# A linear-attention and MoE kernel: TensorE's order fixed by hand, the state product row-tiled, and exp left in PSUM

## The chip, the cores and the metric

The kernel runs on one core of one Trainium2 chip. The metric is the device time in microseconds (us). "Before" is the tuned kernel that the change starts from, "after" is the kernel with the change. A *unit* is one piece of MoE work of about 0.65 us on TensorE: 6 matmuls of 256 columns, 12 of 128 (both for the first MoE product), or 4 of 384 (for the second).

Engines in the profile: PE is TensorE (PEld its weight loads), DVE is VectorE, ACT is ScalarE, POOL is GpSimd, SP is the engine that issues the loads.

## The reference, cut to what matters

```python
# r, k, v, w: (4 batches, 8 heads, 768 positions, 48); u: (8, 48); moe_w_in: (384, 2048); moe_w_out: (2048, 384)
for t in range(S):                                    # attention with a decaying state
    cur = einsum('bhd,bhe->bhde', u[None] * kt, vt)
    y[:, :, t] = einsum('bhd,bhde->bhe', rt, state + cur)
    state = wt[..., None] * state + einsum('bhd,bhe->bhde', kt, vt)
x = y.transpose(0, 2, 1, 3).reshape(3072, 384)
out = square(maximum(x @ w_in, 0)) @ w_out            # fp32 in and out
```

The kernel cuts the sequence into 24 *steps* of 128 positions (4 batches of 6 chunks). Attention must go step by step within a batch. The MoE part of a step can be done at any time after that step's y exists.

## The kernel before

One step of attention is a chain over four engines. The short names are used in all that follows.

| name | engine | what |
|---|---|---|
| Ln, v_bf | ScalarE | logarithm of w; v to bf16 |
| c | TensorE | prefix sums of the logarithms in PSUM |
| exp, rdec | ScalarE, VectorE | exp of c; r and k times their decays |
| ku, qprod, q, vq | GpSimd; q on VectorE | the "bonus" with u; q is a row sum |
| t, rkT | TensorE, VectorE | transposes; eviction of them |
| p, pmT | TensorE, VectorE | scores; two masked evictions |
| s, t_state, S | TensorE, VectorE, GpSimd | state product and state update |
| y, y_sb | TensorE, VectorE | output; eviction with the bonus added |
| x, xT | TensorE, ScalarE | transposes of y; eviction into the MoE's input |

A MoE unit of the first product is evicted by ScalarE (relu, `rl`) and squared by VectorE (`gt`). The parts that the change touches, cut:

```python
def cast_wi(g):
    nc.vector.tensor_copy(wi_sb[:, :, g * GW:(g + 1) * GW], w_st.pop(("i", g))[:])
...
load_wi(0); load_wi(1); load_wi(2); load_wi(3)      # 3 MB of moe_w_in ahead of step 1's inputs
loads[1] = attn_load(1)
...
def st_cum(step):                                   # c, exp, rdec
    ...
    nc.tensor.matmul(cs[:, 0, 0:DM], tri_strict[:], lw[:, :, 0:D], start=True, stop=True)
    nc.tensor.matmul(cs[:, 1, 0:DM], tri_incl_neg[:], lw[:, :, 0:D], start=True, stop=True)
    exps = a_mid.tile([C, 2, H, D], BF16, name="exps")            # exp goes to SBUF
    nc.scalar.activation(exps[:]..., cs[:, :, 0:DM], AF.Exp)
    nc.vector.tensor_mul(rdec[:, :, :, 0:D], st["rk_raw"][:], exps[:])
...
def st_su(step):                                    # state: a 96 x 96 product per pair of heads, masked
    ...
    nc.gpsimd.tensor_mul(am[:], bmask[:], a_c[:, :, None].to_broadcast([C, HP, 2 * D]))
    nc.vector.tensor_add(t_state[:], st["S"][:], su_view)
    nc.gpsimd.tensor_mul(S_new[:], t_state[:], am[:])
...
for t in range(NSTEP):                              # the order is a wish; a scheduler sorts every engine's queue at build time
    ...
    st_prep(t + 1); st_cum(t + 1)
    fill(3); st_p(t); st_bonus(t + 1)
    fill(3); st_tr(t + 1)
    fill(2); st_y(t); st_su(t + 1)
    fill(2); st_yt(t); ready(t); fill(2)            # fill(n): up to n MoE units, if there are any
```

## Time and profile before

Four runs: 237.1, 237.66, 237.76 and 238.68 us. What matters:

| | before |
|---|---|
| span of the profiled run | 235.5 us |
| TensorE busy | 192.9 us (82%) |
| VectorE / ScalarE / GpSimd busy | 165.1 / 126.4 / 118.9 us |
| first MoE matmul | 26.27 us |
| last y transpose | 215.84 us |

The page of the kernel before: busy time by engine; then three rows of its 40 slices of the span (5.9 us each, in tenths busy, and the granted clock in tenths, shown as 9 also where the trace has no clock record yet); then groups of instructions (line, engine, operation, output<-inputs, shapes, count | busy us, mean ns of one | idle time of the engine before them and what ended it).

```profile
PE 192.9 (82%) x1944; PEld 139.2 (59%) x1944; DVE 165.1 (70%) x271; ACT 126.4 (54%) x241; POOL 118.9 (50%) x125
...
PE   0124787889696779969998998999999999999983
...
DVE  3297429999979688486779879788787775753500
...
PEclk9999999999799979967999999999999999999999
...
L277 DVE TENSOR_TENSOR gt<-rl 128x512 bf16<-128x512 f16 x96 | 52.8, 568 | 17.4 <-ACT rl L276 17.0
...
L208 POOL TENSOR_TENSOR am<-bmask,a_c 128x384 f32<-128x384 f32 x20 | 17.2, 858 | 37.2 <-ACT a_c L206 37.2
...
L216 POOL TENSOR_TENSOR S<-t_state,am 128x384 bf16<-128x384 f32 x20 | 23.4, 1168 | 6.1 <-DVE t_state L214 5.4
...
L178 DVE TENSOR_TENSOR rdec_buf_157<-rk_raw,exps 128x768 bf16<-128x768 f32 x8 | 10.6, 1328 | 4.1 <-ACT exps L175 3.3
```

TensorE is full (9, with an 8 now and then) only from the 19th slice on. The state's two GpSimd groups are L208 and L216. One third of the rdec products (L178) took 1328 ns on average; over all 24 they range from 947 to 1745 ns.

The view by stretches of 20 us (columns: stretch; its length; busy time and count of PE, PEld, DVE, ACT, POOL; granted clock; DMA share; GB/s):

```profile
20.00:40.00 20.00, 14.25 (x153) 10.78 (x150) 11.19 (x19) 12.80 (x19) 8.87 (x10) 1.00 1.07 261
40.00:60.00 20.00, 17.12 (x217) 13.14 (x215) 19.47 (x31) 14.14 (x28) 18.04 (x18) 1.00 1.22 180
60.00:80.00 20.00, 17.09 (x164) 11.87 (x164) 17.65 (x27) 10.72 (x22) 14.02 (x14) 0.91 1.11 199
80.00:100.00 20.00, 16.88 (x166) 11.80 (x166) 12.77 (x23) 10.25 (x21) 14.18 (x14) 0.91 0.97 177
100.00:120.00 20.00, 17.56 (x150) 12.22 (x150) 14.86 (x24) 10.26 (x20) 10.52 (x11) 0.83 0.52 106
```

Each stretch of 20 us holds 14 to 17.6 us of busy TensorE, and the granted clock falls to 0.83 in the last.

**How much is lost, and where.** Useful TensorE work is about 176 us: 192 unit equivalents of 0.65 us and 24 steps of 2.1 us (the sum of a step's matmuls, read from the trace). This is an estimate from trace durations. A stretch's loss is its length less the useful work done in it, where a step's 2.1 us are counted whole, when its y transposes run. (To count every matmul at its own start instead moves up to 2.8 us from one stretch to the next.) For the kernel before: 24.2 us until 26.5 us, 9.2 until 50, 5.6 until 80, 12.9 until 130, 7.7 after that; 59.6 in all.

### The profile page before, as it was taken

Reading aid. Unit: us, or ns where it says so; the run is one execution under the profiler, and the core shown is the slowest. Engines: PE = TensorE matmul, PEld = TensorE weight load, DVE = VectorE, ACT = ScalarE, POOL = GpSimd, SP = SyncE. Lnnn points to the kernel's source line nnn. Section 1 sums busy time; section 2 is a strip of 40 time slices with the busy share of each in tenths; the row PEclk is TensorE's granted clock in tenths of the full one; section 3 lists DMA queues with packets and bytes.
Section 4 is the critical chain, followed back from the end, with each engine's and each line's share of the span. In section 5 each row is a group of like instructions: output and inputs, shape, how many; then the busy total and the mean of one; then the engine's idle time right before and its main releaser. Section 6 shows DMA issues by size and latency. Waiting matters only on the chain. (4 is left out here: it accounts for less than half of the span.)

```text
span 235.5 us, 5074 instructions
## 1 busy us (share of the span) xinstructions
PE 192.9 (82%) x1944; PEld 139.2 (59%) x1944; DVE 165.1 (70%) x271; ACT 126.4 (54%) x241; POOL 118.9 (50%) x125
## 2 busy tenths in 40 slices
PE   0124787889696779969998998999999999999983
PEld 0023655658475448646756766678677686776741
DVE  3297429999979688486779879788787775753500
ACT  2203785758376436644654745767566574652710
POOL 4355335898586866747349596783224505200000
PEclk9999999999799979967999999999999999999999
DMA  8999989999999999524694195540101101010101
GB/s 139 339 313 301 334 170 191 170 198 188 173 218 173 203 212 198 119 56 101 130 202 71 43 225 73 114 90 33 36 0 36 36 3 67 0 36 35 34 33 67
DMA packets 107175, 30.40 MB, mean 129 GB/s; under 512 B 100368, under 2 KB 105616, under 8 KB 107152
## 3 DMA queue, kind: packets, MB, share of 16 engines
q1 hardware_dynamic: 107152, 30.09, 62.0%
q8 instruction: 15, 0.25, 0.5%
q14 instruction: 8, 0.07, 0.1%
HBM read 25.36 MB, written 4.72 MB: 128 GB/s over the span
## 5 line engine op out<-in xcount | busy, mean ns | idle before, releaser
L272 PEld LDWEIGHTS <-wi_sb 128*128 128x128 bf16 x624 | 59.0, 102 | 17.5 <-issue 9.6
L277 DVE TENSOR_TENSOR gt<-rl 128x512 bf16<-128x512 f16 x96 | 52.8, 568 | 17.4 <-ACT rl L276 17.0
L287 PEld LDWEIGHTS <-gt 128*128 128x128 bf16 x384 | 36.3, 99 | 23.4 <-issue 4.0
L208 POOL TENSOR_TENSOR am<-bmask,a_c 128x384 f32<-128x384 f32 x20 | 17.2, 858 | 37.2 <-ACT a_c L206 37.2
L166 POOL TENSOR_TENSOR vq<-v_raw,q 128x384 f32<-128x384 f32 x24 | 24.3, 1013 | 22.6 <-DVE y_sb L248 17.5
L230 DVE TENSOR_TENSOR pmT<-cp,tri_strict 128x512 bf16<-128x512 f32 x48 | 30.9, 681 | 4.7 <-PE cp L227 4.7
L161 POOL TENSOR_TENSOR ku<-rk_raw,u_bc 128x384 f32<-128x384 f32 x24 | 26.9, 1121 | 13.8 <-DMA rk_raw<-in_k_dram 9.0
L162 POOL TENSOR_TENSOR qprod<-rk_raw,ku 128x384 f32<-128x384 f32 x24 | 26.4, 1099 | 2.8 <-DVE q L164 1.0
L216 POOL TENSOR_TENSOR S<-t_state,am 128x384 bf16<-128x384 f32 x20 | 23.4, 1168 | 6.1 <-DVE t_state L214 5.4
L175 ACT ACTIVATE exps<-cp 128x768 bf16<-128x768 f32 x24 | 19.5, 813 | 10.6 <-PE cp L173 10.4
L164 DVE TENSOR_REDUCE q<-qprod 128x8 f32<-128x384 f32 x24 | 13.1, 547 | 14.0 <-POOL qprod L162 10.9
L155 ACT CAST v_bf<-v_raw 128x384 bf16<-128x384 f32 x24 | 12.2, 509 | 11.7 <-PE y L244 6.0
L188 DVE COPY rkT<-tr 128x1024 bf16<-128x1024 bf16 x24 | 16.4, 683 | 0.9 <-PE tr L187 0.7
L241 PE MATMUL y<-v_bf,pmT 128*128 128x48 bf16 x192 | 13.9, 187 | 3.6 <-DVE pmT L230 3.5
L256 ACT COPY xT<-y 128x384 bf16<-128x384 bf16 x24 | 11.5, 478 | 8.5 <-PE y L255 7.9
L241 PEld LDWEIGHTS <-pmT 128*128 128x128 bf16 x192 | 11.5, 98 | 6.6 <-DVE pmT L230 5.0
L248 DVE TENSOR_TENSOR y_sb<-vq,y 128x384 bf16<-128x384 f32 x24 | 13.2, 549 | 1.2 <-PE y L244 1.2
L206 ACT ACTIVATE a_c<-su 128x4 f32<-128x4 f32 x20 | 3.4, 170 | 19.6 <-PE su L202 19.6
L178 DVE TENSOR_TENSOR rdec_buf_159<-rk_raw,exps 128x768 bf16<-128x768 f32 x8 | 9.5, 1188 | 5.9 <-ACT exps L175 5.9
L178 DVE TENSOR_TENSOR rdec_buf_157<-rk_raw,exps 128x768 bf16<-128x768 f32 x8 | 10.6, 1328 | 4.1 <-ACT exps L175 3.3
L255 PE MATMUL y<-ident,y_sb 128*128 128x128 bf16 x72 | 8.5, 231 | 5.2 <-DVE y_sb L248 5.1
L227 PE MATMUL cp<-rkT 64*128 64x128 bf16 x192 | 10.5, 231 | 1.8 <-ACT exps L175 1.8
(299 smaller groups left out, 383.9 us busy)
## 6 DMA issues: line engine op xcount, KB each, us to landing
w_raw<-in_w_dram SPq DMA_DIRECT2D x24, 192.0 KB, 4.3
rk_raw<-in_r_dram SPq DMA_DIRECT2D x24, 192.0 KB, 4.3
rk_raw<-in_k_dram SPq DMA_DIRECT2D x24, 192.0 KB, 4.5
v_raw<-in_v_dram SPq DMA_DIRECT2D x24, 192.0 KB, 4.2
out_dram<-o_sb SPq DMA_DIRECT2D x24, 192.0 KB, 2.0
w_st<-in_moe_w_in_dram SPq DMA_DIRECT2D x4, 768.0 KB, 8.1
w_st<-in_moe_w_out_dram SPq DMA_DIRECT2D x4, 768.0 KB, 8.2
u_bc<-in_u_dram SPq DMA_DIRECT2D x1, 192.0 KB, 4.5
```

What stands on the lines that cost most here:

```text
L161: nc.gpsimd.tensor_mul(ku[:], st["rk_raw"][:, 1], u_bc[:])
L162: nc.gpsimd.tensor_mul(qprod[:], st["rk_raw"][:, 0], ku[:])
L166: nc.gpsimd.tensor_mul(vq[:], st["v_raw"][:], q[:, :, None].to_broadcast([C, H, D]))
L175: nc.scalar.activation(exps[:].rearrange("p a h d -> p a (h d)"), cs[:, :, 0:DM], AF.Exp)
L178: nc.vector.tensor_mul(rdec[:, :, :, 0:D], st["rk_raw"][:], exps[:])
L208: nc.gpsimd.tensor_mul(am[:], bmask[:], a_c[:, :, None].to_broadcast([C, HP, 2 * D]))
L216: nc.gpsimd.tensor_mul(S_new[:], t_state[:], am[:])
L230: nc.vector.tensor_mul(pmT[:, e], ps_p[:, e].rearrange("p (a t) -> p a t", a=HP), tri_strict[:, None, :].to_broadcast([C, HP, C]))
L241: nc.tensor.matmul(ps_y[:, h, :], st["pmT"][:, e, p, :], st["v_bf"][:, h, :], start=(h == 0), stop=(c == 0), skip_group_check=True)
L272: nc.tensor.matmul(ps1[:, j, :], wi_sb[:, kk, n * 128:(n + 1) * 128], xT[:, kk, t0:t0 + width], start=(kk == 0), stop=(kk == KT - 1))
L277: nc.vector.tensor_mul(hold["gt"][:, g * ng:(g + 1) * ng, :], rl[:], rl[:])
L287: nc.tensor.matmul(ps2[:], gt[:, n, mt * 128:(mt + 1) * 128], wo_sb[:, n, :], start=(n == 0), stop=(n == NT - 1))
```

## The change

Its intent: keep TensorE fed. TensorE's order is written by hand as a string of stages, with MoE units ("F") between them; the scheduler goes on sorting the other engines. Besides, exp stays in PSUM, the state is kept without its masked half (row-tiled 48-column products), w_in's casts go to ScalarE, and step 1's inputs are loaded before w_in. The core of the diff:

```diff
 def cast_wi(g):
-    nc.vector.tensor_copy(wi_sb[:, :, g * GW:(g + 1) * GW], w_st.pop(("i", g))[:])
+    nc.scalar.copy(wi_sb[:, :, g * GW:(g + 1) * GW], w_st.pop(("i", g))[:])
...
-    load_wi(0) ... load_wi(3)
     loads[1] = attn_load(1)
+    for g in range(4):
+        load_wi(g)
+    loads[2] = attn_load(2)
...
-        exps = a_mid.tile([C, 2, H, D], BF16, name="exps")
-        nc.scalar.activation(exps[:]..., cs[:, :, 0:DM], AF.Exp)
-        nc.vector.tensor_mul(rdec[:, :, :, 0:D], st["rk_raw"][:], exps[:])
+        nc.scalar.activation(a_c[:], cs[:, 0, DM:DM + HP], AF.Exp)
+        nc.scalar.activation(cs[:, :, 0:DM], cs[:, :, 0:DM], AF.Exp)
+        nc.vector.tensor_mul(rdec[:, :, :, 0:D], st["rk_raw"][:], cs[:, :, 0:DM]...)
...
-            nc.tensor.matmul(ps_su[:, p * 2 * D:(p + 1) * 2 * D],
-                             rdec[:, 1, 2 * p:2 * p + 2, :], v_bf[:, 2 * p:2 * p + 2, :], ...)
-        nc.gpsimd.tensor_mul(am[:], bmask[:], a_c[:, :, None].to_broadcast([C, HP, 2 * D]))
-        nc.gpsimd.tensor_mul(S_new[:], t_state[:], am[:])
+            for e in range(2):
+                nc.tensor.matmul(ps_su[e * DP:(e + 1) * DP, p, :], rdec[:, 1, 2 * p + e, :],
+                                 v_bf[:, 2 * p + e, :], start=True, stop=True)
+        nc.gpsimd.tensor_mul(S_new[:], t_state[:], st["a_c"][:, :, None].to_broadcast([C, HP, D]))
...
+    blocks = {1: (0, 256), 2: (2 * C, 128), 3: (3 * C, 128)}     # MoE blocks: after step 1, 2, 3, then every second step
+    for step in range(5, NSTEP, 2):
+        blocks[step] = ((step - 1) * C, 256)
...
+    with tc.manual_schedule(engines={nc.tensor.engine}):         # program order for TensorE alone
+        st_prep(0)
+        run("c0 t0 p0 s0 i0 c1 i1 y0 t1 x0 p1 s1 i2 y1 i3 x1 O0 O1 O2 O3")      # i, o: casts of w_in, w_out; O: loads of w_out
+        ahead(PF - 1)
+        run("F F F F F F c2 F F t2 o0 p2 s2 o1 y2 o2 x2 o3 F F F F F F F F c3 F F F F t3 s3")
+        for t in range(3, NSTEP):
+            f = ["F F"] * 4 if t > 8 else ["F F", "F F", "F F", "F"] if t > 5 else ["F"] * 4 if t == 3 else ["F", "", "F", ""]
+            run(f"c{t + 1} {f[0]}" + (f" x{t - 1}" if t > 3 else "") +
+                f" {f[1]} t{t + 1} p{t} {f[2]} s{t + 1} {f[3]} y{t}")
...
```

An F with no unit at hand does nothing.

More of the change, by code (lines that the diff above doesn't have):

```diff
@@ L45 @@
     PF = 8
+    LAG = 2
     nc.scalar.preload_act_table_set("natural_log_exp_and_others")
@@ L59 @@
     ps_cp = ctx.enter_context(tc.tile_pool(name="ps_cp", bufs=1, space=PSUM))
+    ps_y_pool = ctx.enter_context(tc.tile_pool(name="ps_y", bufs=1, space=PSUM))
     ps_tr_pool = ctx.enter_context(tc.tile_pool(name="ps_tr", bufs=1, space=PSUM))
-    ps_y_pool = ctx.enter_context(tc.tile_pool(name="ps_y", bufs=1, space=PSUM))
-    ps_su_pool = ctx.enter_context(tc.tile_pool(name="ps_su", bufs=1, space=PSUM))
     ps_m1 = ctx.enter_context(tc.tile_pool(name="ps_m1", bufs=2, space=PSUM))
@@ L111 @@
                     ap=[[0, C]] + [list(x) for x in u.ap]))
-    load_wi(0)
-    load_wi(1)
-    load_wi(2)
-    load_wi(3)
     loads[1] = attn_load(1)
+    for g in range(4):
+        load_wi(g)
+    loads[2] = attn_load(2)
     tri_strict = consts.tile([C, C], BF16)
@@ L126 @@
     nc.vector.memset(ones_col[:], 1.0)
-    bmask = consts.tile([C, HP, 2 * D], FP32)
-    nc.vector.memset(bmask[:], 0.0)
-    nc.vector.memset(bmask[0:DP, :, 0:D], 1.0)
-    nc.vector.memset(bmask[DP:C, :, D:2 * D], 1.0)
     NLW = 3
@@ L146 @@
     states = {}
+    S_of = {}
     def st_prep(step):
@@ L171, in st_cum @@
         cs = ps_cp.tile([C, 2, 512], FP32, name="cp")
+        for p in range(HP):
+            nc.tensor.matmul(cs[:, 0, DM + p:DM + p + 1], lw[:, 2 * p:2 * p + 2, :],
+                             ones_col[:], start=True, stop=True)
         nc.tensor.matmul(cs[:, 0, 0:DM], tri_strict[:], lw[:, :, 0:D], start=True, stop=True)
         nc.tensor.matmul(cs[:, 1, 0:DM], tri_incl_neg[:], lw[:, :, 0:D], start=True, stop=True)
-        exps = a_mid.tile([C, 2, H, D], BF16, name="exps")
-        nc.scalar.activation(
-            exps[:].rearrange("p a h d -> p a (h d)"), cs[:, :, 0:DM], AF.Exp)
+        a_c = st["a_c"] = a_small.tile([C, HP], FP32, name="a_c")
+        nc.scalar.activation(a_c[:], cs[:, 0, DM:DM + HP], AF.Exp)
+        nc.scalar.activation(cs[:, :, 0:DM], cs[:, :, 0:DM], AF.Exp)
         rdec = st["rdec"] = rdec_bufs[step % NRD]
-        nc.vector.tensor_mul(rdec[:, :, :, 0:D], st["rk_raw"][:], exps[:])
+        nc.vector.tensor_mul(
+            rdec[:, :, :, 0:D], st["rk_raw"][:],
+            cs[:, :, 0:DM].rearrange("p a (h d) -> p a h d", h=H))
     def st_tr(step):
         st = states[step]
-        rdec, lw = st["rdec"], st["lw"]
+        rdec = st["rdec"]
         ps_tr = ps_tr_pool.tile([C, 2, HP, C], BF16, name="tr")
         rkT = st["rkT"] = a_mid.tile([C, 2, HP, C], BF16, name="rkT")
-        for i in (1, 0):
+        for i in range(2):
             for p in range(HP):
@@ L191, in st_su @@
         st = states[step]
-        rdec, lw, v_bf = st["rdec"], st["lw"], st["v_bf"]
+        rdec, v_bf = st["rdec"], st["v_bf"]
         c = step % NCH
@@ L195, in st_su @@
             return
-        ps_su = ps_su_pool.tile([C, 512], FP32, name="su")
-        fc = HP * 2 * D
+        ps_su = ps_tr_pool.tile([C, HP, D], FP32, name="tr")
         for p in range(HP):
-            nc.tensor.matmul(ps_su[:, fc + p:fc + p + 1], lw[:, 2 * p:2 * p + 2, :],
-                             ones_col[:], start=True, stop=True)
-        for p in range(HP):
-            nc.tensor.matmul(ps_su[:, p * 2 * D:(p + 1) * 2 * D],
-                             rdec[:, 1, 2 * p:2 * p + 2, :], v_bf[:, 2 * p:2 * p + 2, :],
-                             start=True, stop=True)
-        a_c = a_small.tile([C, HP], FP32, name="a_c")
-        nc.scalar.activation(a_c[:], ps_su[:, fc:fc + HP], AF.Exp)
-        am = a_mid.tile([C, HP, 2 * D], FP32, name="am")
-        nc.gpsimd.tensor_mul(am[:], bmask[:], a_c[:, :, None].to_broadcast([C, HP, 2 * D]))
-        t_state = a_mid.tile([C, HP, 2 * D], FP32, name="t_state")
-        su_view = ps_su[:, 0:fc].rearrange("p (a e) -> p a e", a=HP)
+            for e in range(2):
+                nc.tensor.matmul(ps_su[e * DP:(e + 1) * DP, p, :], rdec[:, 1, 2 * p + e, :],
+                                 v_bf[:, 2 * p + e, :], start=True, stop=True)
+        t_state = a_mid.tile([C, HP, D], FP32, name="t_state")
         if c == 0:
-            nc.vector.tensor_copy(t_state[:], su_view)
+            nc.vector.tensor_copy(t_state[:], ps_su[:])
         else:
-            nc.vector.tensor_add(t_state[:], st["S"][:], su_view)
-        S_new = a_mid.tile([C, HP, 2 * D], BF16, name="S", bufs=3)
-        nc.gpsimd.tensor_mul(S_new[:], t_state[:], am[:])
-        states.setdefault(("S", step + 1), S_new)
+            nc.vector.tensor_add(t_state[:], S_of[step][:], ps_su[:])
+        S_new = a_mid.tile([C, HP, D], BF16, name="S", bufs=3)
+        nc.gpsimd.tensor_mul(S_new[:], t_state[:],
+                             st["a_c"][:, :, None].to_broadcast([C, HP, D]))
+        S_of[step + 1] = S_new
     def st_p(step):
@@ L236, in st_y @@
         c = step % NCH
-        ps_y = ps_y_pool.tile([C, H, D], FP32, name="y")
-        for p in range(HP):
-            for e in range(2):
-                h = 2 * p + e
-                nc.tensor.matmul(ps_y[:, h, :], st["pmT"][:, e, p, :], st["v_bf"][:, h, :],
-                                 start=(h == 0), stop=(c == 0), skip_group_check=True)
-            if c > 0:
-                nc.tensor.matmul(ps_y[:, 2 * p:2 * p + 2, :], st["rkT"][:, 0, p, :],
-                                 st["S"][:, p, :], start=False, stop=True,
-                                 skip_group_check=True)
+        ps_y = ps_y_pool.tile([C, 2, 512], FP32, name="y")
+        S = S_of.pop(step, None)
+        for e in range(2):
+            for p in range(HP):
+                nc.tensor.matmul(ps_y[:, e, p * D:(p + 1) * D], st["pmT"][:, e, p, :],
+                                 st["v_bf"][:, 2 * p + e, :],
+                                 start=(p == 0), stop=(c == 0), skip_group_check=True)
+        if c > 0:
+            for p in range(HP):
+                for e in range(2):
+                    rows = slice(e * DP, (e + 1) * DP)
+                    nc.tensor.matmul(ps_y[:, e, p * D:(p + 1) * D], st["rkT"][rows, 0, p, :],
+                                     S[rows, p, :], start=False, stop=True,
+                                     skip_group_check=True)
         y_sb = st["y_sb"] = a_mid.tile([C, H, D], BF16, name="y_sb")
-        nc.vector.tensor_add(y_sb[:], st["vq"][:], ps_y[:])
+        nc.vector.tensor_add(
+            y_sb[:].rearrange("t (p e) d -> t e p d", e=2),
+            st["vq"][:].rearrange("t (p e) d -> t e p d", e=2),
+            ps_y[:, :, 0:HP * D].rearrange("t e (p d) -> t e p d", p=HP))
     def st_yt(step):
@@ L252, in st_yt @@
         y_flat = st["y_sb"][:].rearrange("p h d -> p (h d)")
-        ps_yt = ps_y_pool.tile([C, KT, C], BF16, name="y")
+        ps_yt = ps_tr_pool.tile([C, KT, C], BF16, name="tr")
         for kk in range(KT):
@@ L297, in moe_block @@
                 [m2(mt, qd) for mt in range(width // 128) for qd in range(4)])
-    blocks = [(0, 128, 0), (128, 128, 1)]
-    blocks += [(s * C, 256, s + 1) for s in range(2, NSTEP, 2)]
-    q1 = deque()
-    q2 = deque()
-    waiting = deque()
-    def fill(n):
-        for _ in range(n):
-            if q1 and (not q2 or fill.turn % 3 != 2):
-                q1.popleft()()
-            elif q2:
-                q2.popleft()()
-            else:
-                return
-            fill.turn += 1
@@ L315 @@
-    fill.turn = 0
-    def ready(step):
-        for (t0, width, last) in blocks:
-            if last == step:
-                while waiting:
-                    q2.extend(waiting.popleft())
-                m1s, m2s = moe_block(t0, width)
-                q1.extend(m1s)
-                waiting.append(m2s)
-    def get_S(step):
-        if ("S", step) in states:
-            states[step]["S"] = states.pop(("S", step))
-    st_prep(0)
-    st_cum(0)
-    st_bonus(0)
-    cast_wi(0)
-    st_tr(0)
@@ L336 @@
-    st_su(0)
-    for g in range(1, 4):
-        cast_wi(g)
-    for g in range(4):
-        load_wo(g)
-    for s in range(2, PF):
-        loads[s] = attn_load(s)
-    for t in range(NSTEP):
-        nxt = t + 1 < NSTEP
-        if t + PF < NSTEP:
-            loads[t + PF] = attn_load(t + PF)
-        if nxt:
-            st_prep(t + 1)
-            get_S(t + 1)
-            st_cum(t + 1)
-        if t == 1:
-            for g in range(4):
-                cast_wo(g)
-        fill(3)
-        st_p(t)
-        if nxt:
-            st_bonus(t + 1)
-        fill(3)
-        if nxt:
-            st_tr(t + 1)
-        fill(2)
-        st_y(t)
-        if nxt:
-            st_su(t + 1)
-        fill(2)
-        st_yt(t)
-        ready(t)
-        fill(2)
@@ L369, with fill @@
-    while q1 or q2 or waiting:
-        if not q1 and waiting:
-            q2.extend(waiting.popleft())
-        fill(1)
+    blocks = {1: (0, 256), 2: (2 * C, 128), 3: (3 * C, 128)}
+    for step in range(5, NSTEP, 2):
+        blocks[step] = ((step - 1) * C, 256)
+    fills = deque()
+    coming = deque()
+    flush = [True]
+    held = deque()
+    def fill(_):
+        if not fills and coming:
+            fills.extend(coming.popleft()[1])
+        if not fills and held and flush[0]:
+            fills.extend(held.popleft())
+        if fills:
+            fills.popleft()()
+        if coming:
+            coming[0][0] -= 1
+            if coming[0][0] <= 0:
+                fills.extend(coming.popleft()[1])
@@ new lines, in finish, with ahead @@
+    def finish(step):
+        st_yt(step)
+        if step in blocks:
+            m1s, m2s = moe_block(*blocks[step])
+            old = held.popleft() if held else []
+            held.append(m2s)
+            units = []
+            for i in range(max(len(m1s), len(old))):
+                units += m1s[i:i + 1] + old[i:i + 1]
+            coming.append([LAG, units])
+    asked = [3]
+    def ahead(last):
+        while asked[0] <= min(last, NSTEP - 1):
+            loads[asked[0]] = attn_load(asked[0])
+            asked[0] += 1
@@ new lines, in cum, with tr, su @@
+    def cum(step):
+        if step < NSTEP:
+            st_cum(step)
+            if step + 1 < NSTEP:
+                st_prep(step + 1)
+            if step > 1:
+                ahead(step + PF)
+    def tr(step):
+        if step < NSTEP:
+            st_tr(step)
+            st_bonus(step)
+    def su(step):
+        if step < NSTEP:
+            st_su(step)
+    ops = {"c": cum, "t": tr, "p": st_p, "s": su, "y": st_y, "x": finish,
+           "F": fill,
+           "i": cast_wi, "o": cast_wo, "O": load_wo}
@@ new lines, in run @@
+    def run(text):
+        for tok in text.split():
+            ops[tok[0]](int(tok[1:] or 0))
+    with tc.manual_schedule(engines={nc.tensor.engine}):
[3 more added lines that the diff above has]
+        run("F F F F F F c2 F F t2 o0 p2 s2 o1 y2 o2 x2 o3 F F F F F F F F c3 F F F F t3 s3")
+        flush[0] = False
+        for t in range(3, NSTEP):
+            f = ["F F"] * 4 if t > 8 else ["F F", "F F", "F F", "F"] if t > 5 else ["F"] * 4 if t == 3 else ["F", "", "F", ""]
+            run(f"c{t + 1} {f[0]}" + (f" x{t - 1}" if t > 3 else "") +
+                f" {f[1]} t{t + 1} p{t} {f[2]} s{t + 1} {f[3]} y{t}")
+        run(f"F F x{NSTEP - 1}")
+        flush[0] = True
+        while fills or held or coming:
+            fill(0)
```

## The prediction

> **What bounds it now.** The page's first part gives TensorE 192.9 us busy of a 235.5 us span, VectorE 165.1, ScalarE 126.4, GpSimd 118.9. Pure TensorE work is less: in the timeline one MoE unit (6 matmuls of 256 columns or 4 of 384) advances the array 0.65-0.66 us, and 192 unit equivalents make 126 us; one attention step, read from the chain of waits, is 0.33 (prefix sums) + 0.45 (transposes) + 0.27 (state) + 0.35 (scores) + 0.55 (y) + 0.17 (y transposes) = 2.1 us, 51 us for 24. That is 177 us, 7.4 us a step, the old kernel's pace from 164 to 216 us. Its loss is earlier: the first MoE matmul starts at 26.3 us, and each 20 us from 20 to 120 us hold 14-17.6 us of busy TensorE. Waits there: y transposes for y_sb, transposes for rdec, y for pmT, and MoE matmuls for ScalarE's relu, itself behind VectorE's squares where MoE-in units come in a bunch. The granted clock was 0.91, 0.91 and 0.83 between 60 and 120 us: about 6 us.
>
> **What the change does.**
> 1. Start: step 1's inputs (landed near 18-20 us) go ahead of the 3 MB of w_in, and w_in's casts (4 x 1.75 us) leave VectorE for ScalarE. I expect the first MoE matmul near 22-23 us, of a 256-wide block.
> 2. Order: a fixed round of c FF x FF t p FF s FF y: one MoE-in and one MoE-out unit cover each latency (exps + rdec about 2 us; rkT 0.68; two pmT 1.3; y_sb 0.55; xT 0.48). Rounds with t > 8 hold 8 units; rounds 3 to 8 hold fewer, so there DMA and latency bind, some 6 us each. The tail after the last step is about 17 us of MoE.
> 3. exp stays in PSUM: rdec reads one SBUF operand instead of two. In the trace, VectorE operations with a PSUM operand don't spread (pmT 0.674-0.692); rdec does (0.947-1.745). The Trainium skill ("GPSIMD Engine Reference", specifications) names contention of GpSimd with VectorE instructions having two SBUF inputs; this trace agrees. I expect rdec at 0.96 against 1.23: 6-7 us of VectorE.
> 4. State: am's 17 us of GpSimd vanish, S halves (1.17 to 0.6), t_state 0.55 to 0.35. Little is critical.
> 5. Row-tiled state product: 8 matmuls of 48 columns for 4 of 96; TensorE work about unchanged.
> Cost: tr, su and yt share one PSUM bank, so t waits for the xT copy, s for rkT, x for t_state; the fills hide most.
>
> **Sum.** 23 us start, plus 173 us of TensorE left, is 196; plus 3 us of cold clock, 7-9 us of latency in rounds 2 to 8, 3-4 us of stalls later, 3-5 us of throttle, 3 us of end, 2 us outside the span: about 216 us. The gain of some 20 us comes nearly all from keeping TensorE fed between 23 and 130 us.
>
> **Right or wrong.** Right: first MoE matmul at 22-24 us; rounds of 7.4-7.7 us from t = 9; the last y transpose near 195-198 us; TensorE waits above 1 us only before 85 us; rdec near 0.96 and am gone; VectorE near 150 us. Wrong if rounds stretch beyond 8 us (VectorE, then sets the pace: t waiting for rdec, y for pmT), if inputs arrive late (prefix sums waiting for the logarithm), or if a denser TensorE draws a lower clock.
>
> **Time:** 216 us, range 207 to 227; faster 0.95, within 2% 0.03, slower 0.02.

## The result

The kernel after takes 234.17 us (median of 4 runs, 234.05 to 234.28) against 237.71 for the kernel before in the same rounds. The ratio is 0.985, 95% interval 0.981 to 0.988: a small gain, within 2%. Here and below a ratio is the mean time of one kernel's fast runs over that of the kernel before in the same rounds, so it is not quite the ratio of the medians quoted. Executions over 1.5% slower than the fastest of the same kernel are left out of the means.

The page of the kernel after, the same rows:

```profile
PE 194.8 (84%) x2120; PEld 141.3 (61%) x2120; DVE 143.0 (61%) x264; ACT 131.4 (57%) x249; POOL 81.2 (35%) x105
...
PE   0145694794787999989999999999999999999984
...
DVE  2244356235567688796879878987677756753210
...
PEclk9999997589569999999999999999999999999999
...
L277 DVE TENSOR_TENSOR gt<-rl 128x512 bf16<-128x512 f16 x96 | 48.1, 509 | 34.2 <-ACT rl L276 33.8
...
L208 POOL TENSOR_TENSOR S<-t_state,a_c 128x192 bf16<-128x192 f32 x20 | 10.5, 525 | 72.6 <-DVE t_state L206 56.3
...
L177 DVE TENSOR_TENSOR rdec_buf_159<-rk_raw,cp 128x768 bf16<-128x768 f32 x8 | 7.6, 952 | 6.5 <-ACT cp L175 5.1
```

The arithmetic did what it should: VectorE went from 165.1 to 143.0 us, GpSimd from 118.9 to 81.2, L216's 1168 ns of the state became L208's 525 ns and the mask product is gone, and rdec takes some 950 ns with no spread (943 to 956 over all 24). TensorE is full from the 14th slice on instead of the 19th. But slices 7 to 12 are thinner as a whole than they were (39 tenths busy in sum against 47), and there the clock is down to 5 tenths. The view by stretches says the same:

```profile
20.00:40.00 20.00, 13.85 (x128) 9.97 (x128) 9.73 (x19) 14.74 (x21) 3.28 (x4) 0.94 1.02 253
40.00:60.00 20.00, 15.16 (x139) 10.78 (x140) 7.65 (x16) 9.47 (x19) 11.32 (x13) 0.76 1.22 186
60.00:80.00 20.00, 15.91 (x209) 11.52 (x209) 13.70 (x25) 10.12 (x22) 10.95 (x13) 0.79 1.13 197
80.00:100.00 20.00, 18.89 (x221) 13.73 (x220) 16.31 (x33) 13.40 (x28) 10.52 (x14) 1.00 1.18 203
100.00:120.00 20.00, 19.07 (x223) 14.10 (x222) 16.63 (x31) 11.44 (x24) 10.73 (x12) 1.00 0.80 156
```

Between 40 and 80 us the granted clock is 0.76 and 0.79. In the trace the clock is at half rate in two intervals, 37.6 to 47.8 and 58.1 to 68.3 us; before, in three short ones that sum to 13.7 us (61.2 to 64.6, 85.0 to 88.5, 102.1 to 108.9). The timeline of TensorE in the kernel after (start, busy us, engine, line, operation, count, then [idle before it <- what ended the idle time]) shows one of these places:

```profile
51.10 2.76 PE L287 MATMUL m_663<-wo_sb,gt 128*128 128x384 bf16 x16 [0.15 <-ACT o_sb L291]
...
55.08 0.31 PE L200 MATMUL tr<-v_bf,rdec_buf_155 128*64 128x48 bf16 x8 [0.78 <-DVE rkT L189]
55.33 0.25 PE L169 MATMUL cp<-ones_col,lw_buf_151 128*128 128x1 bf16 x4
...
58.26 1.03 PE L188 MATMUL tr<-ident,rdec_buf_157 128*128 128x128 bf16 x8 [2.33 <-DVE rdec_buf_157 L177]
59.22 0.61 PE L220 MATMUL cp<-rkT 64*128 64x128 bf16 x8
...
64.89 1.03 PE L188 MATMUL tr<-ident,rdec_buf_159 128*128 128x128 bf16 x8 [1.82 <-DVE rdec_buf_159 L177]
...
66.40 1.46 PE L272 MATMUL m_857<-xT,wi_sb 128*128 128x128 bf16 x12
```

The first line is the last four units that were left. From 55 to 66.4 us there is none, then one (the last line, L272). All else, the lines left out too, is the chain of steps 3 to 5, with waits of 2.33 and 1.82 us for rdec.

The account of losses, by the same rule as above, of the kernels that matter (us lost in each stretch):

| stretch | before | after | best (last run below) |
|---|---|---|---|
| 0 to 26.5 | 24.2 | 22.3 | 17.7 |
| 26.5 to 50 | 9.2 | 11.2 | 11.6 |
| 50 to 80 | 5.6 | **14.8** | 4.5 |
| 80 to 130 | 12.9 | 2.9 | 0.3 |
| 130 to the end | 7.7 | 5.4 | 3.6 |
| sum | 59.6 | 56.6 | 37.7 |

So the hand-made round works: from 80 us on 12.3 us are won. But 11.2 us are given back between 26.5 and 80 us.

The starts of the prefix sums say the same more simply. From step 3's to step 10's, after takes 46.3 us and the best run takes 46.3 us too. But in after these rounds hold 28 units and in the best run 39, and step 3's prefix sum starts at 50.4 us in after and at 40.1 us in the best run. So 10.3 us of late start and 11 missing units of 0.65 us, some 17.5 us together (an estimate from the traces), make up nearly all of the 18.5 us between the two.

### The profile page after: what moved, and what is told of

Read it like the earlier page. It is cut to its first block, busy times and chain, and to the rows that moved or that the text cites. A ratio compares the mean times of both kernels' runs of the same rounds, so it can differ in the third digit from the quotient of the medians.

```text
span 232.5 us, 5432 instructions
## 1 busy us (share of the span) xinstructions
PE 194.8 (84%) x2120; PEld 141.3 (61%) x2120; DVE 143.0 (61%) x264; ACT 131.4 (57%) x249; POOL 81.2 (35%) x105
## 4 chain that ended last, share of the span: by engine, by line
PE 56%; SPq 14%; DVE 8%; DMA 7%; POOL 6%; issue 4%; ACT 3%; POOLq 0%; DVEq 0%; ACTq 0%
SPq L68 13%; PE tr L188 4%; DMA rk_raw<-in_k_dram 4%; PE cp L220 2%; DVE pmT L223 2%; POOL qprod L158 2%; POOL ku L157 2%; DVE rkT L189 2%; DMA u_bc<-in_u_dram 2%; DMA v_raw<-in_v_dram 2%; DVE gt L277 1%; PE y L234 1%; PE tr L255 1%; PE cp L171 1%; PE m_3691 L287 1%
## 5 line engine op out<-in xcount | busy, mean ns | idle before, releaser
L277 DVE TENSOR_TENSOR gt<-rl 128x512 bf16<-128x512 f16 x96 | 48.1, 509 | 34.2 <-ACT rl L276 33.8
L272 PEld LDWEIGHTS <-wi_sb 128*128 128x128 bf16 x624 | 57.2, 102 | 15.4 <-issue 3.4
L208 POOL TENSOR_TENSOR S<-t_state,a_c 128x192 bf16<-128x192 f32 x20 | 10.5, 525 | 72.6 <-DVE t_state L206 56.3
L162 POOL TENSOR_TENSOR vq<-v_raw,q 128x384 f32<-128x384 f32 x24 | 20.0, 833 | 32.8 <-DVE y_sb L245 18.9
L175 ACT ACTIVATE cp<-cp 128x768 f32<-128x768 f32 x24 | 19.2, 799 | 0.5 <-DVE q L160 0.2
L256 ACT COPY xT<-tr 128x384 bf16<-128x384 bf16 x24 | 11.4, 476 | 3.4 <-PE tr L255 3.3
L177 DVE TENSOR_TENSOR rdec_buf_159<-rk_raw,cp 128x768 bf16<-128x768 f32 x8 | 7.6, 952 | 6.5 <-ACT cp L175 5.1
L255 PE MATMUL tr<-ident,y_sb 128*128 128x128 bf16 x72 | 8.6, 234 | 2.4 <-DVE y_sb L245 1.6
L220 PEld LDWEIGHTS <-rkT 64*128 64x128 bf16 x192 | 6.0, 101 | 6.2 <-DVE rkT L189 3.4
L188 PE MATMUL tr<-ident,rdec_buf_157 128*128 128x128 bf16 x64 | 5.7, 242 | 4.7 <-DVE rdec_buf_157 L177 4.7
L255 PEld LDWEIGHTS <-y_sb 128*128 128x128 bf16 x72 | 6.0, 103 | 5.9 <-DVE y_sb L245 2.8
```

What stands on the lines that cost most here:

```text
L162: nc.gpsimd.tensor_mul(vq[:], st["v_raw"][:], q[:, :, None].to_broadcast([C, H, D]))
L175: nc.scalar.activation(cs[:, :, 0:DM], cs[:, :, 0:DM], AF.Exp)
L220: nc.tensor.matmul(ps_p[:, e, p * C:(p + 1) * C], rkT[rows, 1, p, :], rkT[rows, 0, p, :], start=True, stop=True)
L272: nc.tensor.matmul(ps1[:, j, :], wi_sb[:, kk, n * 128:(n + 1) * 128], xT[:, kk, t0:t0 + width], start=(kk == 0), stop=(kk == KT - 1))
L277: nc.vector.tensor_mul(hold["gt"][:, g * ng:(g + 1) * ng, :], rl[:], rl[:])
```

## The experiments

Theories for the missing 18 us: **(A)** the order of the first eight or so steps, on TensorE (units used up early) or on the other engines; **(B)** the half-rate clock by itself; **(C)** late data, as the prediction said for rounds 3 to 8; **(D)** the rounds themselves have a floor. 18 kernels ran, in six sessions, each with runs of the kernel before on the same chip; its medians were 236.79 to 237.54 us. All results were correct except in the two runs that skip loads on purpose. "F" and "D" in the strings are a MoE unit and dummy matmuls.

| run | kernel | median us | ratio to before, 95% |
|---|---|---|---|
| a | old order, new arithmetic | 240.84 | 1.016 [1.011, 1.021] |
| b | new order, old arithmetic | 240.36 | 1.014 [1.010, 1.018] |
| c | after + dummy matmuls | 228.95 | 0.966 [0.962, 0.969] |
| d | after, w_out cast on GpSimd | 240.20 | 1.012 [1.008, 1.016] |
| e | after, units spread | 232.71 | 0.970 [0.960, 0.980] |
| f | after, 24 loads fewer | 238.06 | 1.002 [0.996, 1.008] |
| g | new early order | 238.20 | 1.001 [0.994, 1.008] |
| h | g + dummies | 233.67 | 0.985 [0.978, 0.991] |
| i | after again | 234.48 | 0.987 [0.983, 0.992] |
| j | new order in all rounds | 240.15 | 1.013 [1.009, 1.018] |
| k | j + dummies | 236.26 | 0.996 [0.992, 1.000] |
| l | e + dummies | 235.00 | 0.991 [0.986, 0.995] |
| m | j mended | 222.16 | 0.938 [0.933, 0.943] |
| n | m + dummies | 219.86 | 0.927 [0.922, 0.932] |
| o | m, TensorE by hand only | 226.56 | 0.955 [0.949, 0.960] |
| p | after, all engines by hand | 242.47 | 1.020 [1.013, 1.027] |
| q | m, 24 loads fewer | 222.43 | 0.938 [0.931, 0.945] |
| r | n, casts and one Ln sooner | **215.72** | 0.910 [0.906, 0.914] |

### Each half of the change alone (a, b)

Run a takes the arithmetic and its PSUM pools from after, and order, loads and casts from before. Run b the other way round.

```diff
-# a: exps in SBUF, 96 x 96 state with am          # b: loop of wishes, w_in before step 1, w_in cast on VectorE
+# a: exp in PSUM, row-tiled 48-column state       # b: the hand-made strings, loads and casts of after
```

> The old kernel (order left to the scheduler, loads and casts as before) with the new arithmetic alone: exp kept in PSUM, row-tiled state product, compact state. Theory (the loss of the changed kernel is a starved TensorE between 26 and 97 us that the hand-written order causes): the arithmetic is off the critical path, 0 to -3 us against the old kernel, 235 to 238 us. Rival (the arithmetic, with its shared PSUM bank for transposes, state product and y transposes, costs what the order gains): above 240 us.

> The changed kernel with the old arithmetic (own PSUM bank for the state product, exp copied to SBUF, block-diagonal state with its mask): order, loads and casts are the new ones. Theory: within 2 us of the changed kernel, 233 to 237 us, with the same starved stretch from 26 to 97 us. Rival (shared PSUM bank is the cost): 225 us or less.

Both expectations were missed: run b is above both of its ranges, and run a fell in the range of its rival. Either half alone is some 3 us slower than before; together they are 3.5 us faster. For run b the trace shows why. Waits of TensorE after 80 us in run b (engine, group <- what it waited for: us in total, times, longest):

```profile
PE tr L189 <- DVE rdec_buf L180: 5.4, 5, 1.7
PE y L244 <- DVE pmT L232: 4.4, 5, 1.7
```

and the same two stages in the kernel after:

```profile
PE tr L188 <- DVE rdec_buf_157 L177: 0.6, 1, 0.6
PE y L234 <- DVE pmT L223: 0.6, 2, 0.3
```

With the old arithmetic t waits 5.4 us for rdec and y 4.4 us for pmT; with the new one 0.6 and 0.6. VectorE is 161.1 us busy in run b and 143.0 after. Up to step 10's prefix sum run b is only 0.7 us behind after (97.5 us against 96.8, by its first matmul of 384 columns), so its loss lies in these later rounds. So a fixed round needs a VectorE that keeps its pace, and the cheaper rdec and squares are worth more inside the new order than alone. Why run a loses against before was not followed further. Its trace shows that the waits moved: after 80 us TensorE waits no more for rdec and pmT as in before (0.5 and 0.8 us against 4.2 and 2.2), but for ScalarE's evictions of MoE output and xT (9.1 us against 1.6).

### The clock (c, i)

```diff
-        run("c0 t0 p0 s0 i0 c1 i1 y0 t1 x0 p1 s1 i2 y1 i3 x1 O0 O1 O2 O3")
+        run("c0 D8 t0 D5 p0 s0 i0 D2 c1 i1 y0 D6 t1 D3 x0 p1 s1 i2 y1 D3 i3 x1 D3 O0 O1 O2 O3")
...      # Dn: n matmuls of 384 columns whose result nobody reads; likewise up to round 5
```

> The changed kernel with dummy matmuls of 384 columns, about 70 in all, placed where TensorE waits before 68 us, sized to about 70 percent of each wait. Clock theory (the two half-rate stretches of 10 us each, 37.6-47.8 and 58.1-68.3 us, and the cold start to 30 us are a main cost): half-rate stretches gone, 5 to 8 us faster, 226 to 229 us. Starvation theory (TensorE has no ready work there, so the clock matters only where MoE units run, 42.5 to 47.5 us): 2 to 4 us faster, 230 to 232 us.

228.95 us, granted clock 0.992, one half-rate interval of 3.4 us (56.4 to 59.9 us) in place of 20.5 us of them. The first full clock comes at 15.5 us in place of 30.8. The gain on after is 5.2 us. It is made early: the prefix sums of steps 2, 3 and 10 start 2.9, 4.9 and 5.3 us sooner than in after. So it comes from the cold start and the first half-rate interval, and the second one (58.1 to 68.3 us in after) seems to have cost next to nothing. The Trainium skill ("TensorE: Matmul & The Clock Gate", Part 1) says that the array runs at half clock after an idle window of about 3.4 us and at full clock after a busy one; the intervals between two changes of the clock in these traces are multiples of 3.4 us, which agrees. So theory B holds for about 5 of the 18 us. The control:

> The kernel after the change once more, unchanged, as the control for the three kernels that run beside it, and to see how its time goes with the granted clock from run to run. If the half-rate clock is a cost of its own (in the spread-units run, 1.000 of the clock went with 229.4 us and 0.963 with 234.4 us, the same kernel): 233 to 235 us where the clock is 0.955, about 231 where it is 0.98. If the clock only records idle time: no such relation.

234.48 us again (five runs of 233.15 to 234.72, clock 0.946 to 0.956). The clock did not vary enough between these runs to see a relation. The runs of the kernel before do vary, and there are 46 in the six sessions: one with clock 0.956 took 239.31 us, 21 with 0.978 took 237.22 us on average, three with 0.992 or 0.993 took 236.06. That is about 1 us for each 0.01 of the clock (a fit within the sessions; its correlation is 0.89). It agrees in size with run c, but a relation alone doesn't say which of the two is the cause. A sixth run of i took 474.58 us and is left out as slow; it comes back at the end.

### w_out's casts (d)

```diff
-        nc.scalar.copy(wo_sb[:, g * 4:(g + 1) * 4, :], w_st.pop(("o", g))[:])
+        nc.gpsimd.tensor_copy(wo_sb[:, g * 4:(g + 1) * 4, :], w_st.pop(("o", g))[:])
```

> The changed kernel with the casts of w_out on GpSimd in place of ScalarE. In the changed kernel one such cast (1.47 us) sits between the two exponentials of step 2 on ScalarE, and TensorE waits 2.07 us for step 2's transposes. Theory: 1 to 2 us faster, 232 to 233 us, and exp of step 2 directly after a_c. If ScalarE's queue order matters more than that (it feeds a whole idle stretch): 4 us or more.

A miss: 240.20 us, 6 us slower than after. The timeline of run d, VectorE:

```profile
31.37 5.70 DVE L277 TENSOR_TENSOR gt<-rl 128x512 bf16<-128x512 f16 x4 [0.30 <-ACT rl L276]
36.99 0.94 DVE L177 TENSOR_TENSOR rdec_buf<-rk_raw,cp 128x768 bf16<-128x768 f32 x1
```

and GpSimd in the same run:

```profile
31.93 4.87 POOL L103 CAST wo_sb<-w_st 128x1536 bf16<-128x1536 f32 x3
```

Four squares that take 0.42 us each in the median of this run took 5.70 us while GpSimd cast: the last three took 1.60 to 1.68 us each, as long as one cast (1.65 to 1.66 us). rdec came 1.3 us later than in after (35.70). A square reads two SBUF operands (the same tile twice). The Trainium skill ("GPSIMD Engine Reference", 1. Specifications) says GpSimd shares its SBUF interfaces with VectorE, with contention for VectorE instructions with two SBUF inputs; this trace agrees. The scheduler also sorted other queues anew, so the 6 us are not all from this place.

### Units spread in TensorE's order alone (e, l)

```diff
-run("F F F F F F c2 F F t2 o0 p2 s2 o1 y2 o2 x2 o3 F F F F F F F F c3 F F F F t3 s3")
+run("F F F c2 F F F t2 o0 F p2 F s2 o1 y2 o2 x2 o3 F F c3 F F F t3 F s3 F")
-... ["F"] * 4 if t == 3 else ["F", "", "F", ""]
+... ["F F"] * 4 if t == 3 else ["F"] * 4
```

> The kernel after the change with one thing else: in the hand order for steps 2 to 5, MoE units that stood in one lump (six before the prefix sum of step 2, eight after step 2's y transposes) are spread, so that rounds 3 to 5 have a unit in nearly every slot. Same work, same loads, casts and engines. Theory (the order itself starves rounds 3 to 5 of units, the idle TensorE then meets a half-rate clock): TensorE's idle time between 50 and 80 us falls from 7.3 us to under 4, the second half-rate stretch is shorter, and the time falls by 2 to 5 us, to 229 to 232. Rival (the early rounds are bound by the chain of small stages, whatever stands between): under 1 us gained, 233 to 235, because a unit put into the chain of step 2 delays it as much as it fills.

Two runs at 229.41 and 231.41 us counted as fast, with a clock of 1.000 and 0.985; two at 234.01 and 234.39, with 0.963, counted as slow. The ratio 0.970 is that of the fast ones. The four times go with the clock: at 0.963 run e takes as long as after does at 0.955, so a gain from the spreading itself, beside the clock, is not shown. The profile is of a slow run and is not read here. With dummies as well, and one unit more ahead of y2:

> The kernel after the change with both small edits of earlier runs: units spread over steps 2 to 5 and dummy matmuls in the early waits. If starvation and the clock were two separate causes, their gains (about 2 to 4 and 5.2 us) mostly add: 224 to 227. If spreading the units only helped by keeping the clock: as with the dummies alone, 228 to 230.

A miss: 235.00 us, slower than the dummies alone (228.95). The trace has half-rate intervals again, at 16.9 to 20.4, 54.5 to 61.3 and 88.6 to 92.0 us. The dummies sit where the old waits were; that the waits have moved is the likely reason, but it was not tested. The gains of the two edits don't add, and no more was made of them.

### A first new order of all engines (g, h, j, k): two faults of my own

Here the order of VectorE, ScalarE and GpSimd is fixed too. Each stage is cut into its parts, with a letter for each (these are not the letters of the runs): L Ln, V v_bf, c, r rdec, b ku and qprod, q, t, k rkT, p, m pmT, s, T t_state and S, y, Y y_sb, x, X xT, A and B units of the first and second product, G the squares of units done so far. MoE blocks are 128 wide, so units exist after step 0.

```diff
-with tc.manual_schedule(engines={nc.tensor.engine}):
-    ...                                  # the strings of after
+with tc.manual_schedule(engines={nc.tensor.engine, nc.vector.engine, nc.scalar.engine, nc.gpsimd.engine}):
+    run_early("L0 c0 r0 V0 b0 t0 k0 L1 p0 m0 q0 c1 V1 s0 T0 y0 Y0 b1 x0 X0 r1 "
+              "i0 q1 t1 k1 i1 p1 m1 A0 s1 T1 y1 Y1 x1 X1 A0 G i2 A1 G A1 G i3 G A0 A1 G G "
+              "O0 O1 O2 O3 a7 L2 A0 c2 V2 b2 A1 r2 G q2 t2 k2 o0 p2 m2 s2 T2 y2 Y2 B0 x2 X2 "
+              "A2 A2 G o1 B0 A2 G A2 G o2 B0 G o3 L3 c3 V3 r3 b3 B0 B1 B1 t3 k3 q3 L4 s3 T3 V4 ")
+    for t in range(3, 9):                # j, k, m to r (not p): range(3, 24)
+        ...                              # c r G t k p m F s T q G F y, then L and V of step t + 2
```

> The kernel after the change from step 9 on; before that, another hand order, for all four compute engines and not TensorE alone: Ln before the cast of v at step 0, rkT's eviction before the bonus' row sum, squares kept away from the VectorE chain, MoE blocks 128 wide so that the first units exist after step 0's attention, units in every round from 3 on. Theory (the miss is the order of the first eight steps): the first MoE matmul at 20 to 23 us, the prefix sum of step 10 at 84 to 89 us instead of 96.7, time 219 to 227. Rival (latency of the stages or the cold clock bind the early part whatever the order): 230 or more, with the half-rate stretches still there. 128-wide blocks double the number of weight loads per column, which may cost 1 to 3 us in the later rounds.

> The same kernel as in the run before it, with 384-column dummy matmuls in its early waits, that keep TensorE busy and change no result. If what is left to gain in the early part is the half-rate clock: 3 to 5 us faster than without them (they gained 5.2 us on the kernel after), granted clock 0.99. If the new order already keeps the clock: within 1 us of it.

Run g: 238.20 us, a miss. Its first MoE matmul is earlier (17.4 us), but where the hand order stopped, at step 9, the timeline of TensorE in run g has this:

```profile
109.55 1.03 PE L206 MATMUL tr<-ident,rdec_buf 128*128 128x128 bf16 x8 [4.61 <-DVE rdec_buf L195]
```

The scheduler had put the row sums q of several later steps ahead of rdec in VectorE's queue; several of them waited for GpSimd's qprod (up to 2.13 us). Run h, with dummies, took 233.67 us, 4.5 us less, as expected; the same wait is in it (4.6 us). So j and k go on by hand to the last round.

> The new early order once more, with its one fault mended: there, where the hand order of all engines ended (step 9), the scheduler put the bonus' row sums of several later steps ahead of rdec in VectorE's queue, and TensorE waited 4.61 us in one place and fell to half rate after it. Now the hand order of all four engines goes on to the last round. Theory (the order of the early steps is what the change lacks): the wait is gone, the total of done work at 100 us is at least 55 units of us (50.4 in the kernel after), time 226 to 231, half-rate stretches of about 13 us in all still cost some of it. Rival (the early order is worth nothing, latency binds): 233 or more. A third possibility is that a full hand order costs in the later rounds: then rounds from 9 on take over 7.5 us.

> The kernel before this one with the dummy matmuls in its early waits: the version that is meant to be best. Data of step 3 landed at 39 us and its prefix sum ran at 44; with 21 further steps of 7.3 us and a tail of 12 to 18 us that gives 210 to 220 us as the estimate of a floor. Expected 219 to 226 with a clock of 0.99 or more. If it stays above 229, neither the early order nor the clock is what separates the kernel after from the predicted 216.

240.15 and 236.26 us, misses again. The timeline of TensorE in run k, at one of many such places:

```profile
162.59 0.25 PE L190 MATMUL cp<-ones_col,lw_buf 128*128 128x1 bf16 x4 [0.70 <-ACT lw_buf L158]
```

My string named Ln of the next step last in each round, so every prefix sum waited some 0.7 us for it, 13.0 us in all from 60 us on. By what was expected of k, this spoke against theories A and B; the trace shows a fault of the string instead, and the next run mends it.

### The order mended (m, n)

```diff
-      f"... {f[2]} s{t + 1} T{t + 1} q{t + 1} G {f[3]} y{t} a{t + 1 + PF} L{t + 2} V{t + 2} G"
+      f"... {f[2]} L{t + 2} V{t + 2} s{t + 1} T{t + 1} q{t + 1} G {f[3]} y{t} a{t + 1 + PF} G"
...   # and the casts of w_out a few places sooner: "s2 T2 o1 y2 Y2 B0 x2 X2 B0 A2 o2 A2 G B0 A2 G A2 o3 G B0 L3 c3"
```

> The new order of all engines with two faults of the run before mended: Ln of the step after next stood last in every round of ScalarE's hand order, so that each prefix sum waited 0.7 us for it (12 us in all from 60 to 240 us in the profile of the run with dummies); and the casts of moe_w_out stood behind the units, where TensorE waited 2.04 and 1.38 us. Theory (early order and clock are the cause of the miss): the waits before the prefix sums are gone, prefix sum of step 3 at 41 to 45 us (50.35 in the kernel after), time 222 to 229, half-rate stretches of about 14 us in all left. Rival (a round has a floor above 7.45 us in any order that fixes all engines): above 231.

> The same with dummy matmuls in the early waits. Theory: 3 to 5 us faster than the run beside it, 218 to 225, a granted clock of 0.99 or more, prefix sum of step 3 at 40 to 44 us, the prefix sum of step 10 at 84 to 92 us (96.7 in the kernel after), later rounds of 7.3 to 7.5 us. Rival: above 228, then the miss has another cause than the first ten rounds.

222.16 and 219.86 us. From 80 to 130 us TensorE has no idle gap over 0.1 us in either run (2.2 us of them in after), and rounds take 7.5 us. Theory A holds, theory D falls: a round of about 7.5 us from step 6 or 7 on is to be had. The half-rate intervals shrank without dummies, to two of 3.4 us; the dummies then gain 2.3 us, less than the 3 to 5 expected.

### Which order? (o, p)

```diff
 # o: the order of m
-with tc.manual_schedule(engines={nc.tensor.engine, nc.vector.engine, nc.scalar.engine, nc.gpsimd.engine}):
+with tc.manual_schedule(engines={nc.tensor.engine}):
 # p: the order of after
-with tc.manual_schedule(engines={nc.tensor.engine}):
+with tc.manual_schedule(engines={nc.tensor.engine, nc.vector.engine, nc.scalar.engine, nc.gpsimd.engine}):
```

> The kernel of 222.2 us (the new order of all engines, no dummies) with one word taken back: only TensorE's order is fixed by hand, the same order to the instruction; VectorE, ScalarE and GpSimd are left to the scheduler again, as in the kernel after. If the gain lies in TensorE's own order (MoE units from step 0 on, in every round): 222 to 226. If it lies in the other engines' order (row sums ahead of rdec and rkT, Ln late, casts in the chain): 229 to 236.

> The other half: the kernel after with its own TensorE order, unchanged to the instruction, but VectorE, ScalarE and GpSimd also in the order in which the program names their work. If the other engines' order is what the change lacked: the 2.22 us wait of p(0) is gone, 226 to 231. If TensorE's order is: 232 to 236, or worse, as each square now stands inline in VectorE's queue ahead of the next eviction.

Run o is 226.56 us, between its two ranges. TensorE's instructions run in the same sequence as in m, so TensorE's own order (with the narrower blocks that it needs) is worth 7.6 us against after, and the order of the other engines 4.4 us more. (These are differences across sessions; the ratios to before, which leave the sessions out, give some 7.2 and 4.0 us.) Run p is 242.47 us: to fix the other engines by hand in the order in which after happens to name them is worse than the scheduler's order, by 8 us. To fix an order helps only if the order is made with the waits in view.

What the scheduler's order cost is visible in after itself. VectorE in the kernel after, q of step 1 and then rkT of step 0:

```profile
13.67 0.55 DVE L160 TENSOR_REDUCE q<-qprod 128x8 f32<-128x384 f32 x1 [2.11 <-POOL qprod L158]
14.14 0.68 DVE L189 COPY rkT<-tr 128x1024 bf16<-128x1024 bf16 x1
```

Step 0's transposes were done at 12.65 us, but their eviction rkT stood behind the row sum q of step 1, and q waited 2.11 us for qprod; TensorE's p(0) waited 2.22 us for rkT. ScalarE in the kernel after, step 0:

```profile
6.66 0.51 ACT L151 CAST v_bf<-v_raw 128x384 bf16<-128x384 f32 x1 [4.64 <-DMA v_raw<-in_v_dram]
7.08 0.52 ACT L149 ACTIVATE lw_buf_149<-w_raw 128x384 bf16<-128x384 f32 x1
```

w landed at 3.8 us, but its Ln stands behind the cast of v, which landed at 6.6. The first prefix sum ran at 7.6 us, in the hand order at 4.5. The Trainium skill ("PSUM — Partial Sum Buffer", Engine vs sequencer instructions) says that the queues of ScalarE, VectorE and GpSimd are strict FIFO; these two places agree.

### Late data (f, q)

```diff
-            loads[asked[0]] = attn_load(asked[0])
+            loads[asked[0]] = kept[asked[0] % 3] if asked[0] < 9 else attn_load(asked[0])   # steps 3 to 8 reuse steps 0 to 2: wrong on purpose
```

> The kernel after the change, but steps 3 to 8 take the tiles that steps 0 to 2 loaded, so that 24 of the 96 attention loads are not made (wrong results on purpose, same instructions on all other engines). The prediction's theory (data arrival binds rounds 3 to 8): 5 us or more faster, 226 to 229, the prefix sum of step 9 runs at 84 to 86 us instead of 89. Rival (loads land over 10 us before they are read, so the order and the latency of the stages bind): within 0.5 us of the kernel after, 233.7 to 234.7.

238.06 us, 4 us *slower* with fewer loads. VectorE in run f:

```profile
35.17 0.55 DVE L161 TENSOR_REDUCE q<-qprod 128x8 f32<-128x384 f32 x1 [1.22 <-POOL qprod L159]
...
38.05 0.55 DVE L161 TENSOR_REDUCE q<-qprod 128x8 f32<-128x384 f32 x1 [1.67 <-POOL qprod L159]
...
41.09 0.55 DVE L161 TENSOR_REDUCE q<-qprod 128x8 f32<-128x384 f32 x1 [1.84 <-POOL qprod L159]
41.56 0.94 DVE L178 TENSOR_TENSOR rdec_buf<-rk_raw,cp 128x768 bf16<-128x768 f32 x1
```

and TensorE in run f:

```profile
42.56 1.03 PE L189 MATMUL tr<-ident,rdec_buf 128*128 128x128 bf16 x8 [7.36 <-DVE rdec_buf L178]
```

With data that is there from the start, the scheduler ran still more of the later steps' row sums ahead of rdec of step 2, and t(2) waited 7.36 us. So this run says nothing of the loads, and much of the hazard. Run q asks again with the four engines' order fixed:

> The test of the loads again, made clean: the kernel of 222.2 us, whose four engines have a fixed order, with steps 3 to 8 taking the tiles of steps 0 to 2 (24 loads fewer, wrong results on purpose). The earlier run without these loads was spoilt: the scheduler, seeing the data early, put the row sums of later steps ahead of rdec of step 2, and TensorE waited 7.36 us there. If data arrival binds rounds 3 to 8: 2 us or more faster. If not: 221.5 to 223, the prefix sum of step 3 at 46 to 47 us as before.

222.43 us against 222.16: the attention loads of steps 3 to 8 bind nothing in that order. Theory C falls. (The loads of the first three steps and of the weights were not taken away in any run.) It agrees with after's trace, where the inputs of step 8 had landed at 61.2 us, and its prefix sum ran at 82.1.

### The best version (r)

```diff
-  "... D3 T2 o1 y2 Y2 D3 B0 x2 X2 B0 A2 o2 A2 G B0 A2 G A2 o3 G B0 L3 c3 ..."
+  "... D3 T2 o1 y2 Y2 D3 B0 x2 X2 B0 o2 A2 A2 G B0 o3 A2 A2 L3 G B0 c3 ..."
```

> The kernel of 219.9 us (new order with dummies) with the casts of moe_w_out one unit sooner and the Ln of step 3 ahead of the last unit of step 0's block, which had stood behind it although w of step 3 landed near 36 us: the 3.4 us that TensorE waited for those casts and 1.0 us for the Ln go, the prefix sum of step 3 comes at 40 to 42 us instead of 44.0, time 216.5 to 218.5. If the chain of the first three steps only moves the wait: 219 to 220.

215.72 us (4 runs, 215.40 to 216.00), and faster than the theory said. It beats both kernels: 0.910 of before. Three tokens moved (and one G fewer) gave 4.1 us; in run n TensorE had waited 3.4 us for the casts and 1.0 us for Ln of step 3. The page of run r:

```profile
PE 197.1 (92%) x2719; PEld 149.2 (70%) x2719; DVE 141.6 (66%) x265; ACT 132.6 (62%) x249; POOL 85.6 (40%) x105
...
PE   5769789789799999999999999999999999999983
...
PEclk9999999999999999999999999999999999999999
```

and three stretches of it:

```profile
40.00:60.00 20.00, 17.14 (x217) 11.59 (x218) 13.66 (x23) 10.91 (x25) 9.55 (x12) 1.00 1.09 192
60.00:80.00 20.00, 20.00 (x298) 15.52 (x296) 16.65 (x31) 12.98 (x27) 9.14 (x11) 1.00 1.11 185
80.00:100.00 20.00, 20.00 (x293) 15.89 (x291) 14.83 (x29) 12.95 (x26) 8.74 (x10) 1.00 1.05 198
```

The clock is full from 5.9 us, where its record begins, to the end; TensorE is busy without a gap from 60 to 200 us, and the prefix sum of step 10 runs at 86.4 us (96.7 in after).

## Why the prediction was wrong

The time (216, range 207 to 227, measured 234.17) was wrong, and so was the chance of 0.95 for a gain over 2%. Point by point:

- **What bounds it: right.** "keeping TensorE fed" was the lever. The same arithmetic and the same loads, in a better order (with 128-wide blocks and dummies), give 215.72 us. That this is the predicted 216 is luck: the sum behind the 216 is not the one that run r meets (its first MoE matmul comes at 16.3 us, for one).
- **The sum: slightly wrong as arithmetic.** Its terms (196 + 3 + 7 to 9 + 3 to 4 + 3 to 5 + 3 + 2) give 217 to 222, not 216.
- **Start, "first MoE matmul near 22-23 us": wrong.** It came at 26.52 (26.27 before). The loads were early as predicted; the engines' queues were not in a good order. In run o, with 128-wide blocks, it is at 23.0 us; in run m, with all engines by hand, at 17.6.
- **The step that failed: "Rounds with t > 8 hold 8 units; rounds 3 to 8 hold fewer, so there DMA and latency bind, some 6 us each", put at "7-9 us of latency in rounds 2 to 8", with 3 us of cold clock and 3 to 5 us of throttle.** That is 13 to 17 us for the stretch that the trace puts at 26.5 to 80 us, and it lost 26.0 us (11.2 + 14.8). The rounds 3 to 8 took 5.8 to 7.8 us, 6.9 on average, not far from what was written. What was not counted is, first, how few units they hold: 28 from step 3's prefix sum to step 10's, where 39 fit in the same 46.3 us (run r), some 7 us. Second, step 3 itself began at 50.4 us, where 40.1 was to be had (run r), another 10 us. Dummies (run c, 45.4 us) and the new order (run m, 46.8 us) each bring it forward, so more than one cause has a share; the share of the units lumped ahead of it was not split off. A TensorE that idles so much falls to half clock, 20.5 us of it. The attention loads had no part (run q). Most of the first was to be seen in the string: sixteen units stand ahead of the prefix sum of step 3 and four right after it, and then rounds 3, 4 and 5 have none, one and two.
- **Clock, "3 us of cold clock" and "3-5 us of throttle": right in kind, and not far off in size.** Dummies alone, which leave 3.4 us of half rate and a cold start of 15.5 us, gain 5.2 us (run c) against the 6 to 8 charged. The warning "if a denser TensorE draws a lower clock" was the wrong way round: the clock fell where TensorE was thin.
- **Rounds of 7.4-7.7 us from t = 9: right.** 7.5 us from 135.3 to 195.4 us (8 rounds); one round, from 96.8 us on, took 8.4. Waits above 1 us only before 85 us: right, the longest after 80 us is 0.65.
- **Last y transpose near 195-198 us: wrong,** 210.32, from the lost time above.
- **exp in PSUM, rdec 0.96: right.** 0.95 us. VectorE "near 150" is 143.0; that the squares would gain too (568 to 509 ns) was missed.
- **State, "Little is critical": not settled.** In the new order the old arithmetic as a whole costs 6 us (run b against after), but TensorE's waits there are for rdec and pmT and none for S, and the run doesn't split state from exp.
- **Shared PSUM bank, "the fills hide most": right from 80 us on.** TensorE's idle gaps sum to 1.3 us after 130 us.

Open: what put ScalarE in the way in run a; how run r's gain splits between order and dummies in its last step (r was not run without dummies); and how much of run o's 7.6 us is the narrower block.

## What to carry to other kernels

A hand order of one engine is not an order of the kernel: for each stage on the critical chain, look in the trace at what stands in front of it in the queue of every engine that it passes. Count the filler units per round before trusting a round; where units come into being late, make the blocks smaller and spread them, for a lump now is a hole later, and a hole costs the clock as well. An account of lost time by stretch, before and after, finds in minutes where an expected gain was given back.

## What the Trainium skill lacked or had wrong

- "TensorE: Matmul & The Clock Gate", Part 1: it names an idle window of about 3.4 us as what drops the clock, and gives no busy share for it. In the kernel after, half rate began at 58.1 us with no idle gap longer than 2.33 us around it: a mostly idle window is enough here. TensorE was 25% busy in the 3.4 us before that drop and 32% before the other one (37.6 us); in before it was 39 to 42% before its three drops. Over all runs here the share before a drop was 0 to 61%, and no window of 3.4 us that kept the full clock had under 41%. Interval lengths of 3.4, 6.8, 10.2 and 13.7 us in these runs agree with the page's window.
- The same page: it doesn't say that the clock record may begin late. In after it begins with the first full clock, at 30.8 us, and the profile's row says 9 before. There matmuls of 256 columns followed one another every 213 ns, and after 30.8 us every 109 ns; so the first units took 1.44 to 1.49 us at 26.5 to 29.0 us and 0.81 us at 31.2. A mean clock such as 0.955 leaves the cold start out.
- The 474.58 us run (run i) has no clock record at all, so that its clock of 1.00 means nothing. The second product's matmuls took 676 ns in it, against 326 in run a, and followed one another every 432 ns, against 163 in after: slower than half rate would be. The other engines ran as ever (VectorE 143.4 us busy). The same page warns that clock events can be unreliable and tells of a gate stuck low for over 50 us; no page tells of a whole run like this one, and its cause stays open. The group in run i and in run a:

```profile
L287 PE MATMUL m<-wo_sb,gt 128*128 128x384 bf16 x384 | 190.9, 676 | 1.2 <-ACT o_sb L291 1.2
```

```profile
L287 PE MATMUL m<-wo_sb,gt 128*128 128x384 bf16 x384 | 75.4, 326 | 6.1 <-ACT o_sb L291 5.5
```
